# Up-projection weight differences by columns, and a static order re-planned from new durations

## The chip, the cores and the metric

One NeuronCore of a Trainium2 chip runs the whole kernel in one launch. The metric is device time in microseconds (us), the median of several executions; lower is better. Three executions of the kernel before gave 183.47, 184.42 and 184.43 us, so the median is 184.42.

Engines are named as the profile names them: PE (TensorE matmuls), PEld (its weight loads), DVE (VectorE), ACT (ScalarE), POOL (GpSimd), SP (SyncE, which here only issues DMAs). SPq is SP's queue of DMA issues.

## The reference, cut to what matters

```python
# q, k, v: (4, 8, 768, 64) f32; heads 0, 2, 6 attend to all earlier keys,
# the other five to the first 4 keys and a window of 64
scores = scale * np.matmul(q, k.transpose(0, 1, 3, 2))
scores = np.where(mask[None], scores, -1e9)
a = softmax(scores)                              # over keys
x = np.matmul(a, v).transpose(0, 2, 1, 3).reshape(3072, 512)
h1 = x @ w1                                      # w1, w2: (512, 1024)
h2 = x @ w2
g = np.maximum(h1, h2)
return g @ w_out                                 # w_out: (1024, 512)
```

Attention over four batches is followed by a feed-forward layer whose activation is the larger of two projections.

## The kernel before

**The algebra.** max(h1, h2) is relu(x(w1 - w2)) + x w2, so the kernel computes w12 = w1 - w2 once, in bf16, and needs one up-projection instead of two: out = relu(x w12) w_out + x (w2 w_out). The product w2 w_out (`w2o`) is also made once. Only half of the up-projection's matmuls remain, and in exchange the weights are prepared at the start: loaded as f32, cast, transposed, subtracted.

**Weights.** w1 and w2 come in four chunks of 256 columns, 512 KB each (`load_w1`, `load_w2`, `prepare_w`). For chunk c the kernel does two differences (`subtract(c, two)`, line 893), a bf16 cast of w2 (`cast_w2`), eight transposes on PE (`turn_w2`) and a copy out of PSUM (`take_w2`). In the kernel before, each of the two differences takes two of the four 128-row blocks and all 256 columns of the chunk. An up-projection step `up(b, tg, fc)` uses 128 columns (fc) and all four row blocks, so it needs both differences of chunk fc // 2. Chunk c of w1 lies in one of four staging buffers `qn`; w_out's four chunks (`load_wo`, line 878, `cast_wo`) and then the q and k of the head pairs use the same buffers in turn, so load_wo of chunk c waits for both differences of chunk c, and the loads of pair 4 wait for cast_wo of chunk 0.

**Attention.** Heads go in 16 pairs n = 0 to 15, four per batch. Pairs 0 to 3 (batch 0) are loaded in two halves ("parts") in large DMAs and cast piece by piece (`cast_first_qk`, `cast_first_v`). From pair 4 on, q and k of a pair come in eight DMAs (line 476; pair 4 in four, line 471) and v in two (line 487), all issued by SP in a fixed order; POOL casts q, k and v, and DVE transposes q and k in 32x32 squares (`turn_squares`, line 564; pairs 0 to 4 are transposed on PE, line 550). For pairs with a window head, `mix_k` builds a second key tensor `kx`, and `mix_v` a second value tensor `vx`. Then per tile: `scores` (PE, line 624; `ps`), `exp` (ACT, line 641; `at`), `mask` (DVE, line 663), `weighted` (PE, line 685; `po`), `normalise` (DVE, lines 700 and 702; it frees the PSUM bank of `po`).

**Feed-forward.** For each of four batches: `turn_x` transposes the attention output (for the last batch DVE and 32 small DMAs do it), two halves of eight `up` steps (line 759, four matmuls, `ph`), each followed by `relu` on ACT or DVE, then six output tiles of three `down` steps (line 786, four matmuls each, `pout`), `take_out` and `store`. The last tile is split by columns (line 801).

**What sets the order.** Nothing is scheduled on the chip: every engine runs its instructions in the order of the program and waits at each for what it needs. That order is found while the program is built. The kernel records operations with their dependencies, a cost per possible engine, a rank, a `tail` (time from an end until users may go on) and, for DMAs, a time to issue and to move. `Order.plan` then plays time forward: for ACT, DVE, POOL and SP it takes the ready operation of lowest rank (plus a shift), for PE the first of several lists ("TX", "S", "W", "TQ", "F", "P", "D") whose head is ready. Operations with several possible engines go to the one that the plan finds free. `SEEDS` is a list of random seeds; each shifts the ranks of 1 to 20 operations, and the list as a whole is one fixed order. The list "D" holds filler matmuls that are issued only when nothing else is ready before 33 us.

DVE and POOL can hinder each other: in the plan, an operation marked `port` on DVE and every operation on POOL start no earlier than 0.13 us before the other engine's last such operation ends.

```python
FRONT = "B00 B01 B02 B03 B04 A0 L10 L11 w0 L12 w1 B10 B11 B12 B13 B14 A1 w2 w3 o0 o1 o2 o3"
order.run(("TX", "S", "W", "TQ", "F", "P", "D"), together=("S",), spare=("D",), until=33.0, slack=SLACK, ...)
```

Of the kernel before, what the change touches and what calls it, by code (L numbers as in the profile page):

```python
# [110 lines left out]
def heads_of(slots):  # L111
# [10 lines left out]
WARM, FIRST, FIRST_LOADS = 90, 6, 3  # L122


SEEDS = (
# [6 lines left out]
)  # L132


class Op:


    def __init__(self, engine, cost, emit, deps=(), rank=0, tail=0.12, bank=False, issue=0.55, by="SP", single=False, port=False):
# [3 lines left out]
        self.issue, self.by, self.single, self.port = issue, by, single, port  # L142
        self.end, self.ready, self.users = None, 0.0, []
        self.behind, self.followers = None, []


class Order:


# [56 lines left out]
    def plan(self, names, together=(), spare=(), until=0.0, slack=0.0, begin=None):  # L206
# [67 lines left out]
        t = 0.0  # L274
# [3 lines left out]
        while True:  # L278
# [4 lines left out]
            for e in ("ACT", "DVE", "POOL", "SP"):  # L283
# [6 lines left out]
                for o in sorted(able, key=lambda o: (o.rank + o.shift, o.ready, o.number)):  # L290
                    if o.engine == "DMA":
                        free[e] = t + o.issue
                        start = max(free[e], free["DMA"])
                        free["DMA"] = start + o.cost["DMA"]
                        end = free["DMA"] + 0.75
                    else:
                        shared = e == "POOL" or e == "DVE" and o.port
                        begin = max(t, held["DVE" if e == "POOL" else "POOL"] - 0.13) if shared else t
                        end = begin + o.cost[e]
                        if any(max(free[x], t) + c < end for x, c in o.cost.items() if x != e):  # L300
                            continue
                        free[e] = end
                        if shared:
                            held[e] = end
                    pending.remove(o)
                    steps.append((o, e, None))
                    release(o.followers, t)
                    finish(o, end)
                    done = True
                    break  # L310
# [37 lines left out]
def tile_paired_heads(tc, q, k, v, w1, w2, wo, out, qkf, vf, tab, idle, heads):  # L348
# [541 lines left out]
    def subtract(c, two):  # L890
        def emit(e):
            kcs, cols = slice(2 * two, 2 * two + 2), quarter(c)
            eng[e].tensor_tensor(
                out=w12[:, kcs, cols], in0=T["w1f", c][:, kcs], in1=w2f[:, kcs, cols], op=ALU.subtract,
            )
        return emit
# [32 lines left out]
    def prepare_qk(n, part=0):  # L929
        nb, rank = len(parts_of[n][part]), rank_of(n, part)  # L930
        old, bfrees = take("qb")
        if n < HP:
            for ts in ((0,), (1,)):
                cost = {"POOL": 0.35, "DVE": 0.28, "ACT": 0.36} if len(ts) == 1 else {"POOL": 0.52, "DVE": 0.36, "ACT": 0.52}
                mine = [
                    op(
                        None, cost, cast_first_qk(n, part, hh, ts),
                        [*(first[part][t] for t in ts), *old], rank=rank, port=True,
                    ) for hh in range(2)
# [4 lines left out]
        else:  # L944
# [28 lines left out]
        if "S" in KINDS[n] and part + 1 == len(parts_of[n]):  # L973
            cost = {"DVE": 0.5, "POOL": 0.92} if nb == NB else {"DVE": 0.4, "POOL": 0.6}
            ready.append(op(None, cost, mix_k(n), [*ready], rank=rank, port=True))
        k_ready[n] = [*k_ready.get(n, ()), *ready]

    def prepare_v(n, part=0):
# [3 lines left out]
        if n < HP:  # L982
            mine = [
                op(
                    None, {"POOL": 0.35, "DVE": 0.29}, cast_first_v(n, part, hh),
                    [first[part][2], *done_with["v", n][0]], rank=rank, port=True,
                ) for hh in range(2)
            ]
            first_frees[part][2].extend(mine)
        else:  # L990
            old, frees = take("vn")
            T["vn", n, part] = slot("vn").rearrange("p (h n d) -> p h n d", h=2, d=D)
            loads = [load(0.84, load_v(n, part, hh), [*old, sorted_], issue=0.57) for hh in range(2)]
            mine = [op("POOL", 0.84, cast_v(n), [*loads, *done_with["v", n][0]], rank=rank)]
            frees.extend(mine)
        v_ready[n] = [*v_ready.get(n, ()), *mine]
        if "S" in KINDS[n] and part + 1 == len(parts_of[n]):
            cost = (0.49 if KINDS[n] == "FS" else 0.78) * (1 if nb == NB else 0.7)
            v_ready[n] += [
                op("POOL", cost, mix_v(n, lower), [*mine], rank=rank) for lower in (True, False)  # L1000
            ]
# [36 lines left out]
    def weigh(n, half, rank):  # L1038
# [17 lines left out]
        if p == HP - 1 and b >= SQUARES_FROM:  # L1056
# [6 lines left out]
            if half == 1 or not whole:  # L1063
# [4 lines left out]
                        [*turned[b], *done_with["xt", b][0]], rank=n + 4 * half, issue=0.66,  # L1068
                        by=("SP", "ACT")[a % 2], tail=0.5,
                    ) for g in range(4) for a in range(4)  # L1070
# [13 lines left out]
    def prepare_wo(c, rank):  # L1084
        old, frees = take("qn")
        T["wof", c] = slot("qn")[:, 0:2 * d_model].rearrange("p (e f) -> p e f", e=2)
        o = load(1.4, load_wo(c), old)
        cost = {"ACT": 1.05, "DVE": 0.7, "POOL": 1.2}
        wob_ops.append(op(None, cost, cast_wo(c), [o], rank=rank))
        frees.append(wob_ops[-1])  # L1090
# [670 lines left out]
```

## Time and profile before

| | us |
|---|---|
| time of the profiled execution | 184.63 |
| its span (first to last instruction) | 182.8 |
| median of the three executions | 184.42 |
| PE busy (matmuls 1683) | 171.7 |
| DVE busy | 117.9 |
| ACT busy | 108.3 |
| POOL busy | 66.4 |
| filler matmuls, line 900 (18) | 4.9 |
| last matmul ends | 178.4 |
| granted PE clock | 0.998 |

The page divides the span into 40 slices of 4.57 us, a digit for the busy tenths of each; the digit for DMA is 6 to 9 in slices 2 to 28 (to 128 us) and mostly 0 to 3 after. From the page's chain of work that ended last:

| the chain by line | share of the span |
|---|---|
| PE pout L786 | 23% |
| PE ph L759 | 19% |
| SPq L476 | 9% |
| SPq L1616 | 7% |
| PE ps L624 | 5% |

How to read it: "busy" of PE counts matmuls that are in flight, so idle time is what is left between them. Which engine ended an idle stretch stands in brackets behind an instruction of the timeline: `[0.89 <-DVE kx L421]` means 0.89 us without work, ended by DVE's instruction of line 421 that wrote kx.

### The profile page before, as it was taken

The numbers are of one execution on the slowest core, as the hardware profiler recorded it, in microseconds if no ns is written. First come the engines' busy times: TensorE is split into PE (matmuls) and PEld (weight loads), VectorE is DVE, ScalarE is ACT, GpSimd is POOL, SyncE is SP. The second block draws the span as 40 slices with busy tenths as digits, with TensorE's granted clock in tenths as the row PEclk, the third lists the DMA queues.
The fourth block names the chain that finished last, engine by engine and source line by source line (L and its number), as shares of the span: only waits on it lengthen the run. The fifth ranks groups of instructions, "written<-read, shape, count | busy, mean of one in ns | idle before, by whom it ended". The sixth has DMA issues, their size and how long they took to land.

```text
span 182.8 us, 4751 instructions
## 1 busy us (share of the span) xinstructions
PE 171.7 (94%) x1683; PEld 97.0 (53%) x1683; DVE 117.9 (65%) x265; ACT 108.3 (59%) x163; POOL 66.4 (36%) x108
## 2 busy tenths in 40 slices
PE   6899897989999899999989999999999999999990
PEld 1365564556454455566445655666555545545460
DVE  2687959991397789899798989979767632000000
ACT  3197797866956267875736695899673300526410
POOL 2244687504354955345774356683000000000000
PEclk9999999999999999999999999999999999999999
DMA  5999999699899799799998998999112368312032
GB/s 173 307 266 351 230 322 387 218 308 258 139 171 198 118 196 204 127 192 170 177 191 163 152 194 159 158 346 403 37 57 113 43 64 170 74 73 103 0 117 72
DMA packets 120674, 32.90 MB, mean 180 GB/s; under 512 B 107586, under 2 KB 116546, under 8 KB 120642
## 3 DMA queue, kind: packets, MB, share of 16 engines
q1 hardware_dynamic: 113954, 31.73, 74.6%
q10 hardware_dynamic: 6688, 0.79, 2.9%
q8 instruction: 15, 0.25, 0.6%
q14 instruction: 17, 0.14, 0.3%
HBM read 25.43 MB, written 6.29 MB: 174 GB/s over the span
## 4 chain that ended last, share of the span: by engine, by line
PE 58%; SPq 17%; DMA 12%; DVE 5%; issue 4%; POOL 2%; ACT 0%; POOLq 0%
PE pout L786 23%; PE ph L759 19%; SPq L476 9%; SPq L1616 7%; PE ps L624 5%; PE po L685 4%; DMA w2f<-in_moe_w_dram 3%; DMA vf<-in_v_dram 3%; DMA qkf<-in_q_dram 3%; PE po L866 3%; DMA qkf<-in_k_dram 2%; SPq L487 2%; PE pout L801 1%; DVE kx L421 1%; PE px L718 1%
## 5 line engine op out<-in xcount | busy, mean ns | idle before, releaser
L641 ACT ACTIVATE at<-ps 128x1024 bf16<-128x1024 f32 (+2 forms) x64 | 59.9, 978 | 12.5 <-PE ps L624 12.4
L759 PE MATMUL ph<-xt,w 128*128 128x384 bf16 x256 | 45.8, 326 | 1.1 <-DVE x L702 1.0
L786 PE MATMUL pout<-wob,g 128*128 128x512 bf16 x184 | 44.8, 379 | 0.0
L770 ACT ACTIVATE g<-ph 128x384 bf16<-128x384 f32 x56 | 26.8, 491 | 22.5 <-DMA out_dram<-ot 11.1
L421 POOL CAST qb<-qkf 128x768 bf16<-128x768 f32 (+1 forms) x37 | 24.1, 661 | 32.3 <-DMA qkf<-in_k_dram 17.1
L759 PEld LDWEIGHTS <-w 128*128 128x128 bf16 x256 | 23.6, 98 | 16.8 <-DVE x L702 1.3
L663 DVE TENSOR_TENSOR at<-at,tab 128x1024 bf16<-128x1024 bf16 (+5 forms) x45 | 27.3, 633 | 4.5 <-ACT at L641 4.2
L786 PEld LDWEIGHTS <-g 128*128 128x128 bf16 x184 | 16.7, 98 | 18.2
L702 DVE TENSOR_TENSOR x<-po,rez 128x192 f32 x64 | 22.9, 358 | 2.4 <-DVE x L702 0.2
L564 DVE STREAM_TRANSPOSE qk<-qb 128x768 bf16<-128x768 bf16 x22 | 20.8, 963 | 5.0 <-POOL qb L421 5.0
L786 PE MATMUL pout<-w2o,xt 128*128 128x512 bf16 x92 | 23.7, 380 | 0.0
L685 PEld LDWEIGHTS <-at 128*128 128x128 bf16 x477 | 19.1, 98 | 7.2 <-issue 0.5
L624 PE MATMUL ps<-qk 64*128 64x128 bf16 (+2 forms) x307 | 21.7, 234 | 0.0
L685 PE MATMUL po<-vb,at 128*128 128x65 bf16 x387 | 21.7, 194 | 0.1
L421 DVE COPY ot<-pout 128x512 f32<-128x512 f32 (+1 forms) x4 | 2.5, 625 | 29.3 <-PE pout L801 23.4
L421 POOL CAST vb<-vf 128x768 bf16<-128x768 f32 (+1 forms) x21 | 13.7, 666 | 17.5 <-DMA vf<-in_v_dram 13.2
L624 PEld LDWEIGHTS <-qk 64*128 64x128 bf16 x307 | 11.6, 94 | 13.2 <-issue 10.6
L421 POOL COPY vx<-vb 64x650 bf16<-64x650 bf16 (+3 forms) x24 | 16.3, 682 | 1.2
L419 ACT COPY ot<-pout 128x512 f32<-128x512 f32 (+1 forms) x9 | 5.1, 562 | 16.0 <-PE pout L786 12.0
L786 PEld LDWEIGHTS <-xt 128*128 128x128 bf16 x92 | 8.2, 98 | 8.5 <-issue 0.2
L624 PE MATMUL ps<-qk,kx 64*128 64x128 bf16 x91 | 9.2, 216 | 2.6 <-POOL kx L421 1.7
L772 DVE TENSOR_SCALAR g<-ph 128x384 bf16<-128x384 f32 x8 | 4.4, 555 | 7.0 <-PE ph L759 6.9
(66 smaller groups left out, 152.7 us busy)
## 6 DMA issues: line engine op xcount, KB each, us to landing
vf<-in_v_dram SPq DMA_DIRECT2D x24, 192.0 KB, 3.4
qkf<-in_q_dram SPq DMA_DIRECT2D x44, 96.0 KB, 3.2
qkf<-in_k_dram SPq DMA_DIRECT2D x44, 96.0 KB, 2.4
out_dram<-ot SPq DMA_DIRECT2D x11, 256.0 KB, 2.0
w2f<-in_moe_w_dram SPq DMA_DIRECT2D x4, 512.0 KB, 7.3
qkf<-in_moe_w_dram SPq DMA_DIRECT2D x4, 512.0 KB, 9.0
qkf<-in_moe_w_out_dram SPq DMA_DIRECT2D x4, 512.0 KB, 4.5
out_dram<-w2f SPq DMA_DIRECT2D x8, 256.0 KB, 4.5
```

What stands on the lines that cost most here:

```text
L421: eng[e].tensor_copy(out=out, in_=in_)
L476: dma[e].dma_start(out=dst[64 * hh + a:64 * hh + a + 32].rearrange("p (j e) -> p j e", e=32), in_=src[:, :, a:a + 32].rearrange("o (j p) e ...
L564: nc.vector.transpose(T["qk", n][:, t], T["qb", n, 0][:, t])
L624: nc.tensor.matmul(ps[:, bank, e * 128:(e + wide) * 128], lhsT=lhsT, rhs=qk[rows, 0, i * 128:(i + wide) * 128], start=bank not in begun, s ...
L641: nc.scalar.activation(out=at[:, 0:len(w), 0:w[0]], in_=T["ps", n, t][:, 0:len(w), 0:w[0]], func=ACT.Exp, scale=scale,)
L663: eng[e].tensor_tensor(out=at, in0=at, in1=tbl, op=ALU.mult)
L685: nc.tensor.matmul(po[:, hh, b[-1] - 3 * half, :], lhsT=at[:, bank, e * 128:(e + 1) * 128], rhs=rhs, start=first and (bank, hh, e, b) == m ...
L702: nc.vector.tensor_tensor(out=T["x", b][:, 3 * half:3 * half + 3, bass.ds(heads[PLACES[n][hh]], 1), :], in0=po[:, hh, :, 0:D].unsqueeze(2) ...
L759: nc.tensor.matmul(ph, lhsT=w12[:, kc, fc * 128:(fc + 1) * 128], rhs=xts[b % len(xts)][:, 3 * tg:3 * tg + 3, kc, :], start=(kc == 0), stop ...
L770: nc.scalar.activation(out=g[:, fc, :], in_=ph, func=ACT.Relu)
L786: nc.tensor.matmul(pout, lhsT=lhsT, rhs=rhs, start=(e == 0), stop=(e == len(steps) - 1))
L1616: lambda engine, dst=dst, src=src: engine.dma_start(out=dst, in_=src) for dst, src in pieces
```

## The change

1. `subtract(c, two)` takes all four row blocks and 128 of the chunk's 256 columns, instead of two row blocks and 256 columns. Each `up` step waits for the one difference with its columns instead of for two.
2. The plan's numbers: times for the weight loads per chunk (`W_TAKES`) (0.3 to 1.25 us of tail, 1.4 to 2.7 us of moving, instead of 0.12 and 1.5); 1.2 us more for the first load of pair 4; a tail of 0.8 us for the v loads, 1.2 us instead of 0.5 for the last batch's regrouping; some costs (`cast_first_qk` on DVE 0.345 instead of 0.28 us, `cast_wo` on POOL 1.05 instead of 1.2).
3. The plan's rules: consecutive instructions of ACT, DVE and POOL may overlap by `OVERLAP`; casts of w2 and w_out count as users of the port, `cast_first_qk` no longer does; POOL waits for DVE's port users only for operations marked `shy` (differences, kx, vx and v casts).
4. Another list of seeds.

No arithmetic, no tile, no buffer count and no order of the loads changes; the order of the other instructions, and the engine that some run on, follow from 1 to 4.

```diff
+OVERLAP = {"ACT": 0.1, "DVE": 0.08, "POOL": 0.05}
...
 SEEDS = (
-    5, 9, 27, 48, 60, 85, 90, 92, 141, 244, 295, 346, 388, 452, 533, 547, 611, 628, 706, 735, 736,
...
+    130008, 130017, 130035, 130037, 130043, 130056, 130064, 130081, 130089, 130105, 130120, 130122,
...
-                        shared = e == "POOL" or e == "DVE" and o.port
-                        begin = max(t, held["DVE" if e == "POOL" else "POOL"] - 0.13) if shared else t
+                        other = {"POOL": "DVE" if o.shy else None, "DVE": "POOL" if o.port else None}.get(e)
+                        begin = max(t, held[other] - 0.13) if other else t
                         end = begin + o.cost[e]
                         if any(max(free[x], t) + c < end for x, c in o.cost.items() if x != e):
                             continue
-                        free[e] = end
-                        if shared:
+                        free[e] = end - OVERLAP[e]
+                        if e == "POOL" or e == "DVE" and o.port:
                             held[e] = end
...
+    W_TAKES = ((1.5, 1.07, 1.5, 1.25),) + ((2.7, 0.5, 1.4, 0.3),) + 2 * ((1.4, 0.3, 1.4, 0.3),)
...
     def subtract(c, two):
         def emit(e):
-            kcs, cols = slice(2 * two, 2 * two + 2), quarter(c)
+            cols = slice(256 * c + 128 * two, 256 * c + 128 * two + 128)
             eng[e].tensor_tensor(
-                out=w12[:, kcs, cols], in0=T["w1f", c][:, kcs], in1=w2f[:, kcs, cols], op=ALU.subtract,
+                out=w12[:, :, cols], in0=T["w1f", c][:, :, 128 * two:128 * two + 128],
+                in1=w2f[:, :, cols], op=ALU.subtract,
             )
...
-        loaded = load(1.5, load_w2(c))
+        loaded = load(W_TAKES[c][0], load_w2(c), tail=W_TAKES[c][1])
...
-        o = load(1.5, load_w1(c), old)
+        o = load(W_TAKES[c][2], load_w1(c), old, tail=W_TAKES[c][3])
...
-                None, {"DVE": 0.69, "POOL": 1.27}, subtract(c, two), [o, loaded], rank=rank, port=True,
+                None, {"DVE": 0.69, "POOL": 1.27}, subtract(c, two), [o, loaded], rank=rank, port=True, shy=True,
...
-        cast = op(None, {"DVE": 0.7, "POOL": 1.05}, cast_w2(c), [loaded], rank=rank)
+        cast = op(None, {"DVE": 0.7, "POOL": 1.05}, cast_w2(c), [loaded], rank=rank, port=True)
...
-                (t, hh): load(cost, load_qk(n, part, t, hh), [*qn_old, sorted_], issue=issue)
+                (t, hh): load(cost + (1.2 if (n, t, hh) == (HP, 0, 0) else 0.0), load_qk(n, part, t, hh), [*qn_old, sorted_], issue=issue)
...
-            loads = [load(0.84, load_v(n, part, hh), [*old, sorted_], issue=0.57) for hh in range(2)]
-            mine = [op("POOL", 0.84, cast_v(n), [*loads, *done_with["v", n][0]], rank=rank)]
+            loads = [load(0.84, load_v(n, part, hh), [*old, sorted_], issue=0.57, tail=0.8) for hh in range(2)]
+            mine = [op("POOL", 0.84, cast_v(n), [*loads, *done_with["v", n][0]], rank=rank, shy=True)]
...
-            w = [subs[fc // 2, two] for two in range(2)]
+            w = [subs[fc // 2, fc % 2]]
```

The same work stands as follows on the engines in the two built programs:

| operation | before | after |
|---|---|---|
| differences (line 893) | DVE 6, POOL 2 | DVE 7, POOL 1 |
| casts of w2 | DVE 1, POOL 3 | DVE 2, POOL 2 |
| kx (two copies each) | DVE 6, POOL 6 | DVE 10, POOL 2 |
| casts of q and k of pairs 0 to 3 | DVE 14, ACT 5, POOL 13 | DVE 9, ACT 7, POOL 16 |
| filler matmuls | 18 | 17 |
| take_out | ACT 17, DVE 6 | ACT 19, DVE 4 |

Where the order differs, in the places that the prediction speaks of:

| place | before | after |
|---|---|---|
| DVE, cast of w2's chunk 1 | ahead of kx of pair 2 | behind kx of pair 2 and the first normalise of part 1 |
| chunk 2's differences | both on DVE | one on POOL, between its casts of chunks 2 and 3; one on DVE, ahead of pair 2's normalise |
| chunk 3's differences | one on POOL, one on DVE | both on DVE, behind pair 3's normalise |
| kx of pairs 6, 10, 14 | POOL (pair 10's behind the cast of pair 11's q) | DVE |
| kx of pair 13 | DVE | POOL, behind the cast of pair 14's q |
| PE, ahead of the first scores of pair 4 | | two up steps and one product step more |
| PE, ahead of the first scores of pair 10 | | one down step more |
| PE, behind the first scores of pair 13 | | four down steps and two turn_x more, five weighted less |

More of the change, by code (lines that the diff above doesn't have):

```diff
@@ L122, with __init__ @@
 WARM, FIRST, FIRST_LOADS = 90, 6, 3
+OVERLAP = {"ACT": 0.1, "DVE": 0.08, "POOL": 0.05}
 SEEDS = (
[6 rows of a table removed]
[4 rows of a table added]
 )
 class Op:
-    def __init__(self, engine, cost, emit, deps=(), rank=0, tail=0.12, bank=False, issue=0.55, by="SP", single=False, port=False):
+    def __init__(self, engine, cost, emit, deps=(), rank=0, tail=0.12, bank=False, issue=0.55, by="SP", single=False, port=False, shy=False):
         self.cost = cost if isinstance(cost, dict) else {engine: cost}
@@ L141, in __init__ @@
         self.deps, self.bank = [d for d in deps if d is not None], bank
-        self.issue, self.by, self.single, self.port = issue, by, single, port
+        self.issue, self.by, self.single, self.port, self.shy = issue, by, single, port, shy
         self.end, self.ready, self.users = None, 0.0, []
@@ L933, in prepare_qk @@
             for ts in ((0,), (1,)):
-                cost = {"POOL": 0.35, "DVE": 0.28, "ACT": 0.36} if len(ts) == 1 else {"POOL": 0.52, "DVE": 0.36, "ACT": 0.52}
+                cost = {"POOL": 0.35, "DVE": 0.345, "ACT": 0.36}
                 mine = [
@@ L937, in prepare_qk @@
                         None, cost, cast_first_qk(n, part, hh, ts),
-                        [*(first[part][t] for t in ts), *old], rank=rank, port=True,
+                        [*(first[part][t] for t in ts), *old], rank=rank,
                     ) for hh in range(2)
@@ L974, in prepare_qk @@
             cost = {"DVE": 0.5, "POOL": 0.92} if nb == NB else {"DVE": 0.4, "POOL": 0.6}
-            ready.append(op(None, cost, mix_k(n), [*ready], rank=rank, port=True))
+            ready.append(op(None, cost, mix_k(n), [*ready], rank=rank, port=True, shy=True))
         k_ready[n] = [*k_ready.get(n, ()), *ready]
@@ L984, in prepare_v @@
                 op(
-                    None, {"POOL": 0.35, "DVE": 0.29}, cast_first_v(n, part, hh),
-                    [first[part][2], *done_with["v", n][0]], rank=rank, port=True,
+                    None, {"POOL": 0.35, "DVE": 0.28}, cast_first_v(n, part, hh),
+                    [first[part][2], *done_with["v", n][0]], rank=rank, port=True, shy=True,
                 ) for hh in range(2)
@@ L999, in prepare_v @@
             v_ready[n] += [
-                op("POOL", cost, mix_v(n, lower), [*mine], rank=rank) for lower in (True, False)
+                op("POOL", cost, mix_v(n, lower), [*mine], rank=rank, shy=True) for lower in (True, False)
             ]
@@ L1068, in weigh @@
                         [*turned[b], *done_with["xt", b][0]], rank=n + 4 * half, issue=0.66,
-                        by=("SP", "ACT")[a % 2], tail=0.5,
+                        by=("SP", "ACT")[a % 2], tail=1.2,
                     ) for g in range(4) for a in range(4)
@@ L1087, in prepare_wo @@
         o = load(1.4, load_wo(c), old)
-        cost = {"ACT": 1.05, "DVE": 0.7, "POOL": 1.2}
-        wob_ops.append(op(None, cost, cast_wo(c), [o], rank=rank))
+        cost = {"ACT": 1.05, "DVE": 0.7, "POOL": 1.05}
+        wob_ops.append(op(None, cost, cast_wo(c), [o], rank=rank, port=True))
         frees.append(wob_ops[-1])
```

8 rows, old and new, of the table SEEDS are left out of this document.

## The prediction

> **What bounds the kernel now.** I read the page's busy times first, then a table of busy time by stretches, then who waited for whom, then the timeline around PE's idle places. PE is busy 171.7 of 182.8 us, and its work doesn't change, so only its idle time (and the little filler) can be gained. By stretches:
>
> ```profile
> core 0: us, PE busy (x) PEld busy (x) DVE busy (x) ACT busy (x) POOL busy (x), PEclk, DMA share, GB/s
> 15.00:20.00 5.00, 4.53 (x76) 2.90 (x72) 4.02 (x14) 4.19 (x9) 2.10 (x7) 1.00 1.13 340
> 20.00:25.00 5.00, 4.78 (x62) 2.98 (x62) 4.35 (x12) 4.53 (x6) 4.18 (x10) 1.00 0.95 224
> 25.00:30.00 5.00, 4.11 (x77) 2.60 (x76) 3.56 (x8) 4.11 (x6) 4.76 (x11) 1.00 1.07 373
> 30.00:35.00 5.00, 4.87 (x66) 3.08 (x65) 4.93 (x8) 3.54 (x7) 3.14 (x3) 1.00 0.97 346
> 35.00:40.00 5.00, 4.05 (x48) 2.85 (x45) 4.86 (x12) 3.67 (x7) 0.08 (x1) 1.00 0.67 225
> ...
> 60.00:65.00 5.00, 4.33 (x52) 2.46 (x51) 3.77 (x9) 1.16 (x2) 3.84 (x7) 1.00 0.79 142
> ...
> 90.00:95.00 5.00, 3.94 (x39) 1.99 (x38) 4.78 (x8) 2.05 (x2) 3.98 (x6) 1.00 1.10 198
> ...
> ```
>
> The second column is the stretch, the third PE. Idle there: 0.47 + 0.22 + 0.89 + 0.13 + 0.95 + 0.67 + 1.06 = 4.39 us; every other stretch from 40 to 178.4 us has PE full. So 4.39 us is about all that an order can win behind 15 us. Before that the first loads set the pace (the first v lands at 12.1), and the change leaves them alone. The three large holes:
>
> ```profile
> 26.93 1.18 DVE L421 CAST w2b<-w2f 128x1024 bf16<-128x1024 f32 x1 [1.28 <-DMA w2f<-in_moe_w_dram]
> ...
> 28.89 0.23 PE L624 MATMUL ps<-qk,kx 64*128 64x128 bf16 x2 [0.89 <-DVE kx L421]
> ...
> 32.37 1.04 POOL L421 CAST w2b<-w2f 128x1024 bf16<-128x1024 f32 x1 [1.46 <-DMA w2f<-in_moe_w_dram]
> ...
> 32.86 3.37 DVE L893 TENSOR_TENSOR w<-qkf,w2f 128x512 bf16<-128x512 f32 x3
> ...
> 33.80 1.27 POOL L893 TENSOR_TENSOR w<-qkf,w2f 128x512 bf16<-128x512 f32 x1 [0.40 <-DMA qkf<-in_moe_w_dram]
> ...
> 37.18 0.82 PE L759 MATMUL ph<-xt,w 128*128 128x384 bf16 x4 [0.95 <-DVE x L702]
> ```
>
> At 28.89 PE waits for pair 2's kx, which stands on DVE behind a cast that itself waits 1.28 us for a weight load: head-of-line blocking. At 37.18 it waits for normalise (L702), which is behind three differences that took 3.37 us; a free one takes 0.68 (the fastest of six), so 3.37 - 3 x 0.68 = 1.33 us were lost, while POOL's cast and difference ran. And in the middle:
>
> ```profile
> 85.82 0.83 POOL L421 CAST qb<-qkf 128x768 bf16<-128x768 f32 x1 [1.90 <-DMA qkf<-in_k_dram]
> ...
> 90.50 1.52 POOL L421 COPY kx<-qk 64x320 bf16<-64x320 bf16 x2
> ...
> 92.07 0.23 PE L624 MATMUL ps<-qk,kx 64*128 64x128 bf16 x1 [1.06 <-POOL kx L421]
> ```
>
> Pair 10's k is cast by 86.65, but its kx is done on POOL only at 92.02, behind v, vx and pair 11's q. Last, the list of waits:
>
> ```profile
> PEld L759 <- DVE w L893: 0.5, 2, 0.3
> ```
>
> Up steps wait for differences 0.5 us in all, in two waits.
>
> **The change part by part.**
>
> *Columns.* The differences keep their number (8) and size (512 elements a partition), so 0.68 us on DVE and 1.27 on POOL stay. What an up step gains by needing one instead of two is at most the 0.5 us above; the big hole at 37.18 ends with normalise, which frees a PSUM bank, not with a difference. I count nothing for it. Its cover is the order of PE around it; if runs of 128 columns instead of 256 were slower, DVE, nearly full at 30 to 40 us, would pay it 7 times. No row shows that form; bounds: -0.5 to +0.5.
>
> *The front (15 to 46 us).* The cast of chunk 1 moves behind pair 2's kx: the 0.89 us goes. The holes of 0.13 and 0.95 go as well, since chunk 3's differences move behind normalise. Of 0.69 us at 15 to 25 I take 0.3, the turn of pair 3 that waited for POOL's cast behind a w2 cast that is now on DVE. Sum 2.27. What is late next: chunk 2's difference on POOL. The loads land about 1.35 us apart here (the second w2 chunk at 26.9, the fourth at 32.3, four loads later), so w1's chunk 2 lands near 31.0. POOL, done with its cast of chunk 2 (29.7 + 1.04), starts its difference as soon as DVE's earlier one ends, near 31.1, and runs to 32.4. DVE's difference of that chunk then waits to 32.3, ends at 33.0, pair 2's normalise (0.97) at 33.85, and PE, which would take the bank for the fourth up step at about 32.7, stands 1.15 us. If DVE comes first the price is 0; if POOL's 1.27 counts in full, 1.27. I take 1.15, by the row of 33.80, where POOL came between two of DVE's differences. Front: 2.27 - 1.15 = 1.12 won.
>
> The Trainium skill, "SBUF — State Buffer", section "SBUF: two separate sides", says that DVE and GpSimd lock one port pair for a whole instruction and the loser blocks fully. The trace agrees with 1.33 us lost in the three differences; by the rule the price here would be 1.27 instead of 1.15, and the sum 0.12 worse.
>
> SP is behind the same differences: w_out's chunks 2 and 3 wait for the differences of chunks 2 and 3. In the before, the last w_out load was issued at 36.3 (timeline of SPq) and pair 4's first at 36.94; by the walk chunk 3's differences end near 36.4 (33.85 + relu 0.56 + normalise 0.97 + 2 x 0.68 less overlaps), so the stream of q, k and v that follows starts as before, -1.1 (DVE first) to +1.0. The w_out chunk 2 goes out 2.6 us earlier, which can only help. I take 0.
>
> *The middle.* Pair 6's kx moves from POOL to DVE: of the 0.67 us I take all. Gains until pair 10: 1.12 + 0.67 = 1.79. PE then reaches pair 10's scores, with one down step (0.86) more in front, at 90.75 + 0.86 - 1.79 = 89.8. Its kx on DVE: cast to 86.65, square transpose 0.97 to 87.7, a mask of pair 9 (0.69, some 0.4 more when POOL's v cast holds it) to 88.8, two copies of 0.25 and overhead to 89.4. So no wait: the 1.06 goes, total 2.85. (Were the front 1.15 better, PE would come at 88.7 and wait 0.7: most of it would be lost here.)
>
> *Pair 13.* The new order puts kx of pair 13 on POOL behind v (landings from the casts that they released: 108.0; cast 0.83), two vx copies (0.51 to 1.12 each), the cast of pair 14's q (landed near 110.7; 0.83), and two copies of 0.34 to 0.91: ready at 112.4 to 113.9. PE started these scores at 118.27 before; now four downs (3.45) and two x turns (0.67) stand behind them and five weighted (0.98) less, 3.14 us in all, so it arrives at 118.27 - 2.85 - 3.14 = 112.3 and waits 0.1 to 1.6. I take 0.85, the middle. For small waits at masks that the walk doesn't see, 0.4 (like the two holes of 0.2 at 20 to 25).
>
> Sum: 2.85 - 0.85 - 0.4 = 1.6 us less. The tail behind the last matmul (178.4 to 182.8) is the same code. The profiled execution took 184.63; 184.63 - 1.6 = 183.0. The median shown is 0.2 below that execution, so **182.8** for the median.
>
> **The rivals.**
>
> *The load stream holds everything* (0.24). If pair 10's kx comes no earlier than before (92.0), since the stream is late or DVE is blocked by POOL, only the work moved in front of it counts: 0.86 less 0.4 for small waits, about 184.0. For it: PE is 1.8 us ahead of the old time there while the loads are not. Against it: the 5.4 us between the cast of k and the end of kx were POOL's queue, not the load.
>
> *Pair 13 on POOL makes it slower* (0.17). From its kx at 118.27 - 3.14 = 115.1 on, all that was won is gone. The long ends give 113.9; a stream 1.0 late gives 114.9; a q load that needs 3.5 us to land, as the one issued at 71.97 did in the chain of waits, instead of the 2.4 of the one at 65.92, gives 116.0: 0.9 worse, with the small waits 1.3, about 185.7. For it: four DMA landings and the port in one queue. Against: several long ends must meet.
>
> *The columns do nothing, the order gives all.* This changes no number above; it is a rival for the cause, and the forecast already says so.
>
> *DVE comes first at chunk 2, and the stream 1.1 earlier* (0.12): the stream's start passes to pairs 10 and 13, and the gain is 1.6 + 1.1, about 181.7.
>
> **How the numbers follow.** The forecast as worked out has 0.47. About 0.5% (0.9 us) is what a measurement of this kernel can tell from no change. Faster: the forecast but for the part under 0.9 us (0.40) and the DVE-first case (0.12), and a little of the first rival: 0.55 in all. Slower: the second rival beyond 185.3, 0.17. Same: 0.28. The range reaches from 181.4 (the DVE-first case with some of the small waits gone) to 185.1, and takes in the load stream and half of the way to the slower case; the forecast's own range is 182.0 to 183.7.
>
> **What would show it.** Right: no hole at 28 us; a DVE difference of about 1.75 us near 31.2 beside a POOL one of 1.27 and a hole of about 1.1 us in PE before the fourth up step; kx of pair 10 on DVE by 89.5 and no hole over 0.5 there; a hole before pair 13's scores released by POOL's kx; the last matmul near 176.8. Wrong: a new hole at a place not named here, above all at pairs 5 to 9; pair 4's first load issued after 38; or waits of up steps for L893 before that were larger than the 0.5 us shown.

## The result, and the profile after

The kernel after took 183.74 us in the median of 22 executions (181.13 to 185.81), the kernel before 184.07 beside it (183.02 to 185.9). The ratio is 0.9943, 95% interval 0.9917 to 0.9968: a gain of 0.6%, about 1.05 us. The ratio, here and below, leaves out executions more than 1.5% above the fastest of their kernel, nine of after's and one of before's, because after's fastest lies so low; over all 22 the medians differ by 0.33 us only. So there is a small gain, of about 0.3 or 1 us depending on which executions are counted. The kernel after, taken again without any change, gave 183.83 us (182.62 to 186.2, 12 executions) against 184.81, ratio 0.9961 (0.9917 to 1.0004).

The profiled execution of after is its fastest, 181.13 us, span 179.3. PE's busy time is the same (171.5 us of before's 171.7); its last matmul ends at 175.12 instead of 178.42. The table by stretches, columns as before (the second is the stretch, the third PE):

```profile
core 0: us, PE busy (x) PEld busy (x) DVE busy (x) ACT busy (x) POOL busy (x), PEclk, DMA share, GB/s
15.00:20.00 5.00, 4.71 (x77) 2.94 (x73) 4.09 (x15) 4.51 (x9) 2.76 (x10) 1.00 1.13 341
20.00:25.00 5.00, 4.96 (x65) 3.24 (x64) 4.71 (x12) 4.57 (x7) 0.93 (x3) 1.00 0.88 202
25.00:30.00 5.00, 5.00 (x91) 3.40 (x90) 4.31 (x17) 4.89 (x6) 2.77 (x6) 1.00 1.08 374
30.00:35.00 5.00, 4.70 (x64) 2.95 (x62) 4.15 (x12) 4.33 (x7) 4.18 (x3) 1.00 1.01 363
35.00:40.00 5.00, 5.00 (x46) 3.45 (x45) 4.00 (x7) 4.29 (x8) 0.00 (x0) 1.00 0.85 276
60.00:65.00 5.00, 5.00 (x56) 2.84 (x55) 4.15 (x13) 2.71 (x4) 2.18 (x3) 1.00 0.90 166
65.00:90.00 25.00, 24.57 (x293) 14.19 (x291) 23.56 (x47) 18.64 (x27) 13.54 (x17) 1.00 0.98 170
90.00:95.00 5.00, 5.00 (x58) 2.69 (x52) 3.55 (x10) 3.90 (x5) 2.92 (x4) 1.00 0.97 168
```

Idle at 15 to 40 us is 0.29 + 0.04 + 0.30 = 0.63 us where it was 2.66; the 0.67 at 60 to 65 and the 1.06 at 90 to 95 are gone; 0.43 at masks near 71 us is new. With 0.05 behind 95 us all idle time behind 15 us is 1.11 us (4.40 before), and that difference, 3.29, is the 3.30 by which the last matmul comes earlier. The timeline of the same execution, at the three places that the prediction named:

```profile
29.97 1.28 DVE L895 TENSOR_TENSOR w<-qkf,w2f 128x512 bf16<-128x512 f32 x2
30.58 1.57 POOL L423 CAST w2b<-w2f 128x1024 bf16<-128x1024 f32 x1 [2.25 <-DMA w2f<-in_moe_w_dram]
31.97 0.73 DVE L895 TENSOR_TENSOR w<-qkf,w2f 128x512 bf16<-128x512 f32 x1 [0.71 <-DMA qkf<-in_moe_w_dram]
32.20 1.62 POOL L895 TENSOR_TENSOR w<-qkf,w2f 128x512 bf16<-128x512 f32 x1
32.21 0.62 PE L855 MATMUL pw<-tab,w2b 128*128 128x128 bf16 x8 [0.30 <-POOL w2b L423]
...
87.60 0.42 DVE L423 COPY kx<-qk 64x320 bf16<-64x320 bf16 x2
...
110.33 0.90 POOL L423 COPY kx<-qk 128x320 bf16<-128x320 bf16 x2
```

At chunk 2 DVE's difference began 0.23 us ahead of POOL's (31.97 and 32.20), ran freely (0.73), and POOL paid (1.62 instead of 1.27). This is the first half of the "DVE first" rival, for which the prediction had 181.7; its second half, a stream of loads that starts 1.1 us earlier, did not come (36.84 against 36.94). Pair 10's kx is ready at 88.0, pair 13's at 111.2, and neither is waited for.

The profiled execution of the second sample (182.83 us, span 181.1) had the same front, DVE ahead by 0.04 us at chunk 2, but not the same pair 13; from its timeline:

```profile
112.58 0.84 POOL L423 COPY kx<-qk 128x320 bf16<-128x320 bf16 x2
113.48 0.23 PE L626 MATMUL ps<-qk,kx 64*128 64x128 bf16 x2 [0.85 <-POOL kx L423]
```

Here PE stands 0.85 us for POOL's kx, the figure of the prediction; to the hundredth that is luck, since it was the middle of 0.1 to 1.6. So one program, with its order fixed, has different holes in different executions. The experiments are about which of them belong to the change.

### The profile page after: what moved, and what is told of

Same layout as the page of the kernel before. It is cut to its first block, busy times and chain, and to the rows that moved or that the text cites. A ratio compares the mean times of both kernels' runs of the same rounds, so it can differ in the third digit from the quotient of the medians.

```text
span 179.3 us, 4746 instructions
## 1 busy us (share of the span) xinstructions
PE 171.5 (96%) x1682; PEld 96.9 (54%) x1682; DVE 113.5 (63%) x270; ACT 110.7 (62%) x168; POOL 59.2 (33%) x98
## 4 chain that ended last, share of the span: by engine, by line
PE 77%; DMA 8%; DVE 7%; ACT 2%; issue 2%; POOL 1%; SPq 1%; POOLq 0%
PE pout L788 29%; PE ph L761 23%; PE ps L626 8%; PE po L687 6%; DMA w2f<-in_moe_w_dram 4%; PE po L868 4%; DMA qkf<-in_k_dram 4%; DVE at L665 2%; PE px L720 2%; DVE x L704 2%; ACT at L643 2%; PE ps L600 2%; PE pout L803 1%; DVE qk L566 1%; PE pt L552 1%
## 5 line engine op out<-in xcount | busy, mean ns | idle before, releaser
L761 PE MATMUL ph<-xt,w 128*128 128x384 bf16 x256 | 44.7, 326 | 0.0
L423 POOL CAST qb<-qkf 128x768 bf16<-128x768 f32 (+1 forms) x40 | 25.1, 643 | 35.1 <-DMA qkf<-in_k_dram 16.7
L761 PEld LDWEIGHTS <-w 128*128 128x128 bf16 x256 | 24.1, 98 | 15.6 <-issue 0.4
L665 DVE TENSOR_TENSOR at<-at,tab 128x1024 bf16<-128x1024 bf16 (+5 forms) x45 | 26.2, 609 | 8.8 <-ACT at L643 8.6
L788 PEld LDWEIGHTS <-g 128*128 128x128 bf16 x184 | 16.8, 98 | 18.5 <-issue 0.2
L687 PEld LDWEIGHTS <-at 128*128 128x128 bf16 x477 | 18.2, 98 | 6.4 <-issue 0.6
L423 DVE COPY ot<-pout 128x512 f32<-128x512 f32 (+1 forms) x3 | 1.8, 603 | 30.5 <-PE pout L803 26.5
L687 PE MATMUL po<-vb,at 128*128 128x65 bf16 x387 | 20.7, 194 | 0.3 <-DVE at L665 0.3
L423 POOL CAST vb<-vf 128x768 bf16<-128x768 f32 (+1 forms) x18 | 12.2, 688 | 21.6 <-DMA vf<-in_v_dram 15.0
L423 POOL COPY vx<-vb 64x650 bf16<-64x650 bf16 (+3 forms) x24 | 15.1, 632 | 1.7 <-DVE vb L423 0.5
L702 DVE RECIPROCAL rez<-po 128x6 f32<-128x6 f32 x32 | 5.9, 186 | 5.0 <-PE po L687 4.9
```

The costliest lines, as they stand in the source:

```text
L423: eng[e].tensor_copy(out=out, in_=in_)
L665: eng[e].tensor_tensor(out=at, in0=at, in1=tbl, op=ALU.mult)
L687: nc.tensor.matmul(po[:, hh, b[-1] - 3 * half, :], lhsT=at[:, bank, e * 128:(e + 1) * 128], rhs=rhs, start=first and (bank, hh, e, b) == m ...
L702: nc.vector.reciprocal(out=rez, in_=po[:, :, :, D])
L761: nc.tensor.matmul(ph, lhsT=w12[:, kc, fc * 128:(fc + 1) * 128], rhs=xts[b % len(xts)][:, 3 * tg:3 * tg + 3, kc, :], start=(kc == 0), stop ...
L788: nc.tensor.matmul(pout, lhsT=lhsT, rhs=rhs, start=(e == 0), stop=(e == len(steps) - 1))
```

## The experiments

Twelve runs in three groups of four, each run of 12 executions against 35 of the kernel before, taken with its group on the same chip. The edits move single instructions in the finished order, or change which part of the weights a difference covers. In the first group, `after_again` is the second sample above.

**The kernel after again** (`after_again`), no edit.

> The changed kernel once more, to see a second execution of it and how far its times spread. Theory A (the order is right about the chip): again no hole over 0.3 us in PE behind 25 us, a last matmul within 0.5 us of 175.1, and a median 1 to 3 us below the kernel before. Theory B (the profiled execution, which was the fastest of 22, was a lucky one: DVE took chunk 2's difference ahead of POOL because the weight loads landed 0.8 us later than in the trace of before): now a hole of about 1.1 us before the fourth up step or one at pairs 10 or 13, a last matmul at 176 to 177.5, and a median 0.3 to 1.2 us below the kernel before.

Measured: 183.83 us, 0.9961 (0.9917 to 1.0004). Theory B fits: the hole of 0.85 at pair 13, a last matmul at 176.73, a median 0.98 us below the kernel before (184.81). DVE was first at chunk 2 again, though. Of use is above all its profile, the second one of the same program.

**Columns alone** (`cols_only`): the kernel before with change 1 and nothing else.

```diff
-            kcs, cols = slice(2 * two, 2 * two + 2), quarter(c)
+            cols = slice(256 * c + 128 * two, 256 * c + 128 * two + 128)
```

> The kernel before, in its own order, with the eight differences taken by columns. Each up step still stands where it stood, but its wait is now for one difference. Theory A (the columns give nothing, the order gives all): within 0.3 us of the kernel before, the hole of 0.95 us before the sixth up step still ended by normalise, differences still 0.67 to 0.68 us where nothing blocks them. Theory B (the columns give the gain): 0.5 to 1 us faster, the hole before the sixth up step smaller by as much.

184.65 us, ratio 1.0002 (0.9962 to 1.0043): no change that can be told, with 0.4% open either way. Its timeline shows the collision of before's order at chunk 3:

```profile
34.89 1.27 POOL L893 TENSOR_TENSOR w<-qkf,w2f 128x512 bf16<-128x512 f32 x1 [0.28 <-DMA qkf<-in_moe_w_dram]
34.91 1.79 DVE L893 TENSOR_TENSOR w<-qkf,w2f 128x512 bf16<-128x512 f32 x1 [1.21 <-DMA qkf<-in_moe_w_dram]
37.65 0.66 PE L759 MATMUL ph<-xt,w 128*128 128x384 bf16 x3 [1.64 <-DVE x L702]
```

One load releases both differences. POOL starts 0.02 us earlier, DVE's takes 1.79 instead of 0.68, and PE stands 1.64 us for the normalise behind it. Who is first by 0.02 us is worth over a microsecond here: where DVE came first at this place, in the last experiment below, PE stood 0.24 us.

**The order alone** (`rows_in_after`): the kernel after with pieces by row blocks (the diff above the other way round). The plan still counts one difference for each up step; on the chip the step waits for both.

> The changed kernel, in its own order, with the differences taken by row blocks again, so that each up step waits for both differences of its chunk. Theory A (the columns give nothing): as fast as the changed kernel within 0.3 us. Theory B (the order was found for up steps that wait for one difference, and needs it): the third up step waits for chunk 1's second difference, and the fifth for chunk 2's on POOL; 0.5 to 1.5 us slower than the changed kernel, with new holes before those two up steps.

184.60 us, 1.0026 (0.9993 to 1.006): the whole gain is lost, 0.0065 above the kernel after in the same group. Taken alone this says that the order needs the columns. The timeline shows what happened in one execution:

```profile
23.37 0.68 DVE L895 TENSOR_TENSOR w<-qkf,w2f 128x512 bf16<-128x512 f32 x1
23.50 1.10 PE L761 MATMUL ph<-xt,w 128*128 128x384 bf16 x4
24.10 0.12 PEld L761 LDWEIGHTS <-w 128*128 128x128 bf16 x2 [0.50 <-DVE w L895]
...
30.15 1.03 POOL L423 CAST w2b<-w2f 128x1024 bf16<-128x1024 f32 x1 [1.69 <-DMA w2f<-in_moe_w_dram]
30.47 4.39 DVE L895 TENSOR_TENSOR w<-qkf,w2f 128x512 bf16<-128x512 f32 x3
31.45 1.42 POOL L895 TENSOR_TENSOR w<-qkf,w2f 128x512 bf16<-128x512 f32 x1 [0.26 <-DMA qkf<-in_moe_w_dram]
32.81 1.50 POOL L423 CAST w2b<-w2f 128x1024 bf16<-128x1024 f32 x1
33.47 0.82 PE L761 MATMUL ph<-xt,w 128*128 128x384 bf16 x4 [0.62 <-DVE w L895]
35.80 0.44 PE L761 MATMUL ph<-xt,w 128*128 128x384 bf16 x1 [1.14 <-DVE x L704]
```

The first up step takes 1.10 us instead of 0.81, because its last two row blocks wait for the second difference of chunk 0. PE is 0.3 us later from there on; a normalise and then DVE's differences of chunk 1 come later (30.47 instead of 29.97), and in this execution chunk 2 of w2 landed earlier (POOL's cast at 30.15 instead of 30.58). So POOL's cast is ahead of DVE, POOL's difference follows, and DVE's three take 4.39 us instead of 3 x 0.68: 2.35 us blocked. PE stands 0.62 and 1.14 us. The 0.3 us sit upstream of the race, but that they decided it is not shown: by columns DVE's differences of chunk 1 began anywhere from 29.97 to 30.98 in seven executions, and 30.47 lies among these.

**The cast moved** (`cast_moved`): in the kernel before, DVE's cast of chunk 1 goes behind pair 2's kx.

```diff
+    move(steps, ("cast", 1), ("kx", 2))
```

> The kernel before with one instruction moved: DVE's cast of w2's chunk 1 stands behind kx of pair 2 instead of ahead of it. Theory A (PE's time in the front comes through to the end): the hole of 0.89 us at 28.9 is gone, pair 4's scores start 0.5 to 1 us earlier, and the end is 0.5 to 0.9 us earlier. Theory B (the loads of q and k set the middle): the hole goes, but PE waits as much longer for kx of pairs 6 and 10 as it came earlier, since the last w_out load and with it the loads of pair 4 start no earlier; the end is within 0.2 us of the kernel before.

184.27 us, 0.9952 (0.9909 to 0.9994). That is 0.9 us by the ratio, as theory A has it, but the interval begins at 0.1 us, and the medians of all executions (184.27 and 184.81) differ by 0.54. The hole of 0.89 is gone, but PE then waits 0.50 for a normalise at 30.5 and 0.79 for a difference at 31.9.

The second group: the race forced either way, and the two kx moves.

**DVE first, POOL first** (`dve_first`, `pool_first`): chunk 2's piece on the one engine writes 129 columns instead of 128, so that it has to wait for the other engine's piece.

```diff
+            a, b = 128 * two, 128 * two + 128
+            if (c, two) == (2, 0):     # in dve_first: POOL's piece
+                b += 1
+            if (c, two) == (2, 1):     # in pool_first: DVE's piece
+                a -= 1
+            cols = slice(256 * c + a, 256 * c + b)
```

> The kernel after; chunk 2's difference on POOL takes one more column, which DVE's difference of that chunk writes, so POOL's always comes second. Theory A (the order at this chunk is decided anew by 0.02 to 0.04 us in each execution, and sets the time): every execution is like the profiled one of the kernel after; PE idle at 30 to 36 us at most 0.35, w_out chunk 2 issued near 34, ratio 0.985 to 0.991 of the kernel before, spread smaller than the 3 to 4 us seen. Rival B (the spread comes from elsewhere, and DVE is first nearly always): as the kernel after, 0.994 to 0.997.

> The kernel after; chunk 2's difference on DVE takes one more column, which POOL's writes, so POOL's always comes first. Theory A, with the prediction's price: a hole of 1.0 to 1.3 us in PE before the fourth up step, released by normalise; DVE's differences of chunk 3 and all of the loads from pair 4 on up to 1.0 later; 1.2 to 2.7 us more than with DVE first, ratio 0.997 to 1.004. Rival B (no cost that reaches the end): within 0.003 of the one with DVE first.

DVE first: 183.62 us, 0.9946 (0.9913 to 0.9979). POOL first: 185.14 us, 1.0031 (0.9998 to 1.0065). The difference is 0.0085, 1.57 us: forced, the order at this one chunk is worth more than the whole change. (Forced, POOL first costs PE 2.34 us at 36 us, more than unforced, since DVE comes back so late that POOL's next cast is ahead of it too. And three of the twelve POOL-first executions had a mean granted clock of PE of 0.989 to 0.991, none of the DVE-first ones less than 0.995; without the three the POOL-first median is 184.56.)

But DVE first is no better than the kernel after itself, and its spread is no smaller (182.26 to 186.07): the expectation of 0.985 to 0.991 failed. The times fit rival B, that the kernel after comes out DVE first nearly always. The traces speak against it. From the POOL-first one:

```profile
30.23 2.12 DVE L917 TENSOR_TENSOR w<-qkf,w2f 128x512 bf16<-128x512 f32 x2
30.68 1.13 POOL L440 CAST w2b<-w2f 128x1024 bf16<-128x1024 f32 x1 [2.17 <-DMA w2f<-in_moe_w_dram]
32.02 1.47 POOL L917 TENSOR_TENSOR w<-qkf,w2f 128x512 bf16<-128x512 f32 x1 [0.21 <-DMA qkf<-in_moe_w_dram]
```

POOL's cast comes in between DVE's two differences of chunk 1, the second of which takes 1.52 us and ends at 32.36. POOL's difference of chunk 2 starts at 32.02, when its load lands, so here POOL was first even without being forced. The DVE-first execution begins in the same way (POOL's cast at 30.62, DVE's second difference at 30.91), and POOL was free at 31.89, DVE at 32.43. How often the kernel after comes out DVE first, and why forcing it brings nothing, stays open. The spread has other causes too; the chain of waits of the DVE-first execution shows one:

```profile
82.65 4.72 DMA qkf<-in_k_dram
87.37 0.02 issue
87.39 0.04 POOLq L440
87.43 0.08 issue
87.51 0.84 POOL qb L440
88.35 0.02 issue
88.37 0.98 DVE qk L583
89.35 0.68 DVE at L682
90.03 0.02 issue
90.05 0.56 DVE kx L440 x2
```

Pair 10's last load of k took 4.72 us from issue to landing; in the two profiles of after 2.6. Its kx is ready at 90.6, PE comes with the front's gain, and stands 0.68 us. Pair 13's kx cost 0.85 in this execution as well.

**kx of pair 13** (`kx13_dve`): it goes from POOL back to DVE.

```diff
+    move(steps, ("kx", 13), ("turn", 13, 1), "DVE")
```

> The kernel after; kx of pair 13 goes from POOL to DVE, behind that pair's second square transpose. Theory A (POOL's queue of v, two vx, q and kx costs 0.05 to 0.85 us before pair 13's scores, as two executions showed): that hole goes, nothing comes in its place, ratio 0.002 to 0.004 below the kernel after, so 0.990 to 0.994. Rival B (DVE is full there): a mask of pair 12 comes 0.5 us late instead, same ratio or above, 0.995 to 0.999.

184.90 us, 0.9996 (0.9952 to 1.0041): against theory A, and a little above rival B's range. The profiled execution had lost the race, at a place that the edit doesn't touch:

```profile
29.86 1.06 POOL L439 CAST w2b<-w2f 128x1024 bf16<-128x1024 f32 x1 [0.61 <-DMA w2f<-in_moe_w_dram]
30.98 3.81 DVE L911 TENSOR_TENSOR w<-qkf,w2f 128x512 bf16<-128x512 f32 x3
31.14 1.65 POOL L911 TENSOR_TENSOR w<-qkf,w2f 128x512 bf16<-128x512 f32 x1 [0.22 <-DMA qkf<-in_moe_w_dram]
...
35.73 0.50 PE L777 MATMUL ph<-xt,w 128*128 128x384 bf16 x2 [1.15 <-DVE x L720]
```

These lines begin as the prediction's working does: the load of w2's chunk 2 landed at 29.73 (29.7 was assumed), POOL came first, and PE stood 1.15 us for the normalise before the fourth up step. But normalise ended at 35.67 where the prediction had 33.85, since POOL's difference and then its next cast each held up one of DVE's differences (3.81 us for three), and PE itself came 1.9 us later than assumed. That the hole agrees to the hundredth is luck. At pair 13 no kx is waited for, but PE stands 0.56 for a normalise behind it, much as rival B has it.

**The two kx alone** (`kx_moved`): in the kernel before, kx of pairs 6 and 10 go to DVE.

```diff
+    move(steps, ("kx", 6), ("turn", 6, 1), "DVE")
+    move(steps, ("kx", 10), ("turn", 10, 1), "DVE")
```

> The kernel before; only kx of pairs 6 and 10 go from POOL to DVE, behind the second square transpose of each pair. Theory A (the prediction's middle): the holes of 0.67 and 1.06 us go, a little is lost again at masks: 1.0 to 1.7 us less, ratio 0.991 to 0.995. Rival B (the load stream holds the middle, and what is won at pair 10 is waited for at pairs 11 to 13): 0.997 to 1.001, with a new hole over 0.5 us between 92 and 125 us.

183.75 us, 0.9956 (0.9929 to 0.9984). Both holes are gone; 0.43 us at a mask near 91.6 came in. The gain is 0.8 us, a little under what was expected.

The third group: the race removed, and the parts put together.

**Chunk 2 on DVE** (`chunk2_dve`, `rows_chunk2_dve`, `chunk2_kx13`): POOL's difference goes to DVE behind the normalise, then the same by row blocks, then by columns with kx of pair 13 on DVE too.

```diff
+    o, e, bank = steps.pop(place(steps, ("sub", 2, 0)))
+    at = place(steps, ("sub", 2, 1))
+    later = [k for k in range(at + 1, len(steps)) if steps[k][1] == "DVE"]
+    steps.insert(later[0] + 1, (o, "DVE", bank))
```

> The kernel after; POOL's difference of chunk 2 goes to DVE, behind the normalise that follows DVE's own. Nothing is left to race for there but POOL's cast of chunk 3. Theory A (the race costs the kernel after in a share of its executions): none of them over 185, PE idle at 30 to 36 us at most 0.6, ratio 0.987 to 0.993 of the kernel before. Rival B (DVE is full at 30 to 38 us, the 0.68 more is given back as a later chunk 3, w_out load and pair 4): 0.995 to 1.000.

> The same with pieces by row blocks instead of columns. Theory A (columns are worth something by themselves under this order, since an up step needs one difference and not two): 0.4 to 0.9 us slower than the one with columns, ratio 0.003 to 0.006 higher, with waits of up steps for L895's pieces. Rival B (what the run with row blocks lost was the lost race): within 0.002 of the one with columns.

> Chunk 2 on DVE and kx of pair 13 on DVE as well. Theory A (the run with kx of pair 13 on DVE was slow because POOL came first at chunk 2 in many of its executions): 0.3 to 0.8 us less than with chunk 2 alone, ratio 0.002 to 0.004 lower. Rival B (kx in DVE's row holds masks and normalise of pair 12 up, more than POOL's queue does): 0.002 to 0.004 higher, with a hole of 0.4 to 0.6 released by DVE near 112 us.

183.49 us, 0.9957 (0.9914 to 1.0); by rows 183.51 us, 0.9952 (0.9911 to 0.9992); with kx 183.29 us, 0.9944 (0.991 to 0.9977). With no race at chunk 2, columns are worth nothing that these runs can tell. That fits a lost race as what the order by rows lost before, but with intervals of 0.4% either way it doesn't show it, and by columns the race can be lost too. kx of pair 13 can't be told either way. Of chunk 2 on DVE alone the first expectation failed: it is no faster than the kernel after, and two executions were over 185. In the profiled execution pair 10's k load was late again (3.6 to 3.9 us), and PE stood 0.54 there and 0.6 twice near 112 us.

**Three instructions moved** (`both_moved`): the kernel before with the cast and the two kx moved.

> The kernel before with the cast of chunk 1 behind kx of pair 2, and kx of pairs 6 and 10 on DVE; three instructions moved, no columns, no new order. Theory A (holes add up until the next late thing): 0.9952 and 0.9956 for the parts give 0.990 to 0.992, below the kernel after. Rival B (PE comes to pair 10 that much earlier, and waits for its kx or a mask there): 0.994 to 0.997, with a hole of 0.5 to 1 us between 88 and 93 us.

183.32 us, 0.9932 (0.9894 to 0.997). The parts alone give 0.9952 x 0.9956 = 0.9908; the value lies between that and rival B's, and the interval takes in both. The profiled execution has no hole at pair 10, where one was expected, but two that before's profile doesn't have: 0.93 for a normalise at 16.8, ahead of all that was moved, and 1.06 for a mask at 60.7. At chunk 3, where before's order lost in the other four profiles, DVE came first by under 0.01 us:

```profile
34.40 0.69 DVE L911 TENSOR_TENSOR w<-qkf,w2f 128x512 bf16<-128x512 f32 x1 [0.86 <-DMA qkf<-in_moe_w_dram]
34.41 1.81 POOL L911 TENSOR_TENSOR w<-qkf,w2f 128x512 bf16<-128x512 f32 x1
36.04 0.82 PE L777 MATMUL ph<-xt,w 128*128 128x384 bf16 x4 [0.24 <-DVE x L720]
```

The hole at this place, 0.95 to 1.64 in the four, is 0.24. Nothing here beats the kernel after beyond the intervals, but moving three instructions of the old order brings as much as the new one, as far as these runs can tell.

## Why the prediction was right, and where it wasn't

The direction held, and so did the places where the old order lost time. The time is 183.74 where 182.8 was forecast, inside the range, with about two thirds of the gain (1.05 of 1.6 us by the ratio, 0.33 by all executions). That it came so near is in part luck: both profiles of after show the branch at chunk 2 that the forecast had as a rival, and in the branch that it assumed a second term, the load stream, was off by 2 us.

*Columns.* "I count nothing for it" holds as far as the runs can tell: 1.0002 alone, and no difference by rows without the race. What doesn't fit is the order by rows, 0.0065 slower than by columns. By rows the first up step is 0.3 us longer, upstream of the race, which in that execution went to POOL; PE's idle time at 30 to 40 us was then 1.76 us, against 1.19 in the execution by columns that lost the race (kx of pair 13 moved). How much of the 0.0065 is the rows' own stays open.

*The front.* The holes named went: 2.03 us less idle at 15 to 40 us, 2.27 expected. The price of 1.15 for POOL's difference is what failed as a fixed term. Where POOL comes first PE stood 1.15 in one execution and 0.62 + 1.14 in another; in both profiled executions of after the price is absent. By the traces, what decides is whether POOL's cast of chunk 2 starts, as w2's chunk 2 lands, before or after DVE's second difference of chunk 1. In the four profiles of this order in which both engines were free to come first:

| execution | POOL's cast starts | DVE's second difference starts | first at chunk 2 |
|---|---|---|---|
| after | 30.58 | 30.57 | DVE |
| after again | 30.95 | 30.73 | DVE |
| rows in after | 30.15 | 31.66 | POOL |
| kx of pair 13 moved | 29.86 | 31.57 | POOL |

If DVE's pair is ahead, POOL's cast is held up by it (1.57 and 1.36 us instead of 1.04) and reaches its difference too late to be first. In the fastest execution the lead was 0.01 us. In the five profiles with chunk 2 edited POOL's cast was ahead each time, by 0.15 to 1.50 us. So of nine profiles of this order only after's own two have DVE ahead, and the chance of 0.12 for that rival is not refuted. I took the load's landing, 29.65, from before's trace; in after's two it was 30.45 and 30.82, and DVE's start of chunk 1 moved by as much between executions. A landing time of one execution was used as if it were fixed. No run moved the landing alone, so that it decides is read from traces and not tested.

*The load stream.* Taken as 0, in a walk in which POOL comes first, with bounds of -1.1 and +1.0. The first load of pair 4 was issued at 36.84 and 37.13 in the two profiles of after (36.94 before), where DVE came first. Where POOL came first it was issued at 38.90 (kx of pair 13 moved), 38.97 (rows) and 39.14 (forced). First after, then kx of pair 13 moved:

```profile
36.84 0.92 SPq L473 DMA_DIRECT2D qkf<-in_q_dram  x2
38.90 0.93 SPq L489 DMA_DIRECT2D qkf<-in_q_dram  x2
```

So the term fits only the branch that the forecast didn't assume. In the assumed one it was +2.0 to +2.2, twice the bound, and past the 38 that the prediction itself named as a sign of being wrong. What the walk lacked is POOL's next cast, which holds DVE up a second time: chunk 3's differences ended at 38.22 in the run with kx moved, where the walk had 36.4. The rival in which this stream holds everything finds no support in the two profiles of after. In part it is true in others: pair 10's last k load took over 3.5 us in 8 of the 14 profiles of all kernels, 2.3 to 2.8 in the rest.

*The middle.* 0.67 and 1.06 gone, right, and shown alone (0.9956). kx of pair 10 was ready at 88.0 where 89.4 was expected, and its last k had landed at 83.30 (85.67 before): a second landing time that was taken as fixed. The remark that with a better front PE would come at 88.7 and wait 0.7 has its like in the DVE-first execution, 0.68 up to 90.67; but there the wait came of the late k (landed at 87.37), and both profiles of after, with the better front, have none.

*Pair 13.* Expected ready at 112.4 to 113.9 with a wait of 0.85: 111.2 with no wait for it, 113.4 with 0.85, and 0.85 again at 114.7 with DVE first. It was 0.82 in the POOL-first profile, and at most 0.08 in the three others with this kx on POOL (by rows, and the two with chunk 2 on DVE). So the mechanism is right, but the wait is there in three profiles of seven.

*Small masks.* 0.4 expected, 0.43 and 0.42 measured in the two.

*The sum.* The terms are those of separate executions, and each varies: the race by 1.15 to 1.76 us where it is lost unforced, pair 10's load by 0 to 0.7, pair 13's queue by 0 to 0.85. The profiled execution of after is the one in which all three went well (181.13), before's is an ordinary one. So a step from profile to profile, 3.5 us, says more than three times too much, and the forecast of 1.6 by the same way was 0.5 too much. In what share of its executions the kernel after loses each of the three is not known; only one execution per run has a trace. Why the run with kx of pair 13 moved was slower than the others, while the same move with chunk 2 on DVE wasn't, stays open too.

## What to carry to other kernels

Where two engines share something and the same load releases both, look for the two start times in the trace: if they differ by hundredths, the hole behind them can come and go from one execution to the next, and a forecast has to carry both outcomes. A forecast or an order that takes its landing times from one trace may fit that execution only; compare two or three profiles of the same program before you believe a hole or its absence. And list the few instructions that stand wrongly in a queue before planning anew: here three moves were worth as much as the new plan, as far as the runs can tell.

## What the runs showed of the hardware

In these traces DVE's f32 differences and POOL's casts and differences take turns in the order in which they start, and the wait stands inside the duration. In the run with kx of pair 13 moved, four stand in a row: POOL's difference ends at 32.788, DVE's 0.551 later, POOL's cast 0.897 after that, DVE's next 0.545 after that. So once both have work waiting, DVE's 0.68 becomes 1.5 to 1.8 each time. The Trainium skill, "SBUF — State Buffer", section "SBUF: two separate sides", says that whichever starts first has the shared ports for the whole instruction; the runs agree down to a lead of 0.02 us.

In the run by rows in the order of after, PE's granted clock fell to half for some three microseconds behind the two holes; in the POOL-first run, with a longer hole at the same place, it stayed at full. By stretches, first by rows, then POOL first:

```profile
35.00:36.00 1.00, 0.20 (x1) 0.11 (x2) 0.96 (x3) 0.00 (x0) 0.00 (x0) 0.95 0.91 338
36.00:37.00 1.00, 1.00 (x5) 0.46 (x4) 0.93 (x4) 0.00 (x0) 0.00 (x0) 0.50 0.71 164
...
38.00:39.00 1.00, 1.00 (x5) 0.50 (x4) 0.90 (x2) 0.48 (x1) 0.00 (x0) 0.50 0.29 102
```

```profile
35.00:36.00 1.00, 0.03 (x1) 0.04 (x2) 0.93 (x5) 0.00 (x0) 0.00 (x0) 1.00 0.37 139
36.00:37.00 1.00, 1.00 (x7) 0.61 (x8) 0.93 (x4) 0.17 (x1) 0.00 (x0) 1.00 0.81 287
```

PEclk is the third number from the end. At 0.5 for 36 to 39 us and 0.84 in the next, that execution lost some 1.7 us beyond its holes, by an estimate from these rows (3 x 0.5 + 0.16). None of the other 13 profiles has such a fall in its middle, and that the holes caused this one is not shown; the length of the longest hole doesn't foretell it (1.14 us here, 2.34 us in the POOL-first run).
